# A decode attention kernel: VectorE's 30 middle heads as a loop, and value sums put ahead of the transposes that wait for a load

## Chip, cores, metric

One core of one Trainium2 chip. The metric is the device time of one execution in microseconds. Times before and after are medians. The profile of a kernel is that of one execution, and its span is some 1.8 us below that execution's time: 1927.44 us for the kernel before (a run beside those of the median).

## The reference, cut to what matters

One token (x is 1x640) attends to 32 heads of 32768 cached keys and values of 192 numbers each, in bf16, followed by a small dense block. K and V together are 805 MB, and each byte is used once.

```python
q = (layernorm(x) @ wq).reshape(1, 1, 32, 192).transpose(0, 2, 1, 3)
p = softmax(einsum("bhqd,bhkd->bhqk", q, k_cache) * 192 ** -0.5)      # 32 heads, 32768 keys
h = x + einsum("bhqk,bhkd->bhqd", p, v_cache)....reshape(1, 1, 6144) @ wo
out = h + relu(layernorm(h) @ w1) @ w2
```

## The kernel before

Each head's K and V come in 4 loads of 3 MB each; a load is worked on in two chunks of 32 columns of 128 keys. TensorE (PE) transposes 20 or 16 of the 32 columns, ScalarE (ACT) copies them out of PSUM, PE forms scores; VectorE (DVE) forms the scores of the other 12 or 16 columns by products and sums. ACT takes exponents (`ep`, `ed`), and PE sums the values. SyncE (SP) issues the loads; POOL turns landings into semaphore increments for PE. PE and ACT run heads 1 to 30 as a loop; DVE, POOL and SP are written out for all heads. In the lines of the profile `tp` are the transposes in PSUM (where this kernel puts PE's results), `kT` their copies, `sp` PE's scores, `pr` and `sc` VectorE's products and sums, `pB` and `pA` the exponents of `sp` and of `sc`, `o_ps` the value sums, `qb` the query row. The parts that matter (cuts marked):

```python
# SP: a V load waits for the value sums of the load before the last (2 V buffers, 4 K buffers)
load(kt[ld][:], rows(k_hd, h, ...), f"dk{ld}", "k", h, ld)
if n >= NV:
    hp, lp = divmod(n - NV, NL)
    g.wait("PV", hp, 2 * lp + 1)
load(vt[ld % NV][:], rows(v_hd, h, ...), f"dv{ld % NV}", "v", h, ld)
...
# PE: a new load's transposes (even c) wait for K; the values of the chunk before stand behind them
def pe_head(g, h, turn=None):
    for c in range(NC):
        transposes(g, h, c)
        if c > 0:
            values(g, h, c - 1)
        elif h > 0:
            values(g, h - 1, NC - 1)
            den_mm(g, h - 1)
        scores_pe(g, h, c)
        ...
# DVE: written out
def dve_program(g):
    ...
    for h in range(H):
        for c in range(len(chunks(h))):
            scores_dve(g, h, c)            # waits for the K load itself
            if c == 0 and h > 0:
                den_rec(g, h - 1)
                o_scale(g, h - 1)
            if c == 1 and h > 0:
                o_turned(g, h - 1)         # even h: memset of oT; odd h: a copy
```

The softmax here doesn't subtract the row's maximum and nothing guards it: scores larger than these inputs give would overflow.

## Time and profile before

| | before |
|---|---|
| time, median of the 3 runs then made | 1926.88 us |
| HBM traffic | 825 MB, 428 GB/s over the span, 433 in a good slice |
| PE, DVE, ACT busy | 81%, 80%, 50% |
| DVE instructions in the trace | 979, of which 670 counted as busy work |
| refill packets (the page's kind "instruction", queue q14; DVE's are 8192 bytes and stand 124 to 131 of its instructions apart) | 15 |

The page's view of the DMA issues tells how long a load takes from issue to landing (last column, us). At 433 GB/s a 3 MB load is 7.27 us of work, so 15.5 us says that about one load was still in front of a V load when it was issued.

```profile
kt<-in_A_k_cache_dram SPq DMA_DIRECT2D x127, 3072.0 KB, 22.5
vt<-in_A_v_cache_dram SPq DMA_DIRECT2D x127, 3072.0 KB, 15.5
```

The shares of the chain of waits that ended last:

```profile
DMA 76%; PE 22%; SPq 1%; issue 0%; ACT 0%; POOLq 0%; DVE 0%
```

### The profile page before, as it was taken

How to read it: one execution, taken by the hardware profiler on the slowest of the kernel's cores; microseconds unless marked ns; L12 is line 12 of the kernel's file. 1: busy time of each engine (PE TensorE's matmuls, PEld its weight loads, DVE VectorE, ACT ScalarE, POOL GpSimd, SP SyncE). 2: the span in 40 equal slices, each digit the busy share in tenths (PEclk: the TensorE clock that was granted, in tenths of full speed). 3: DMA queues.
4: the chain of work that ended last, by engine and by line, in shares of the span. 5: the costliest groups of instructions: out<-in, count | busy, mean ns of one | idle time of the engine just before them, and what ended most of it. 6: DMA issues, size and time to landing. Idle time of an engine off the chain costs nothing.

```text
span 1925.6 us, 36082 instructions
## 1 busy us (share of the span) xinstructions
PE 1563.4 (81%) x15899; PEld 1074.8 (56%) x15899; DVE 1546.3 (80%) x670; ACT 970.6 (50%) x2031; POOL 0.7 (0%) x6
## 2 busy tenths in 40 slices
PE   5887888787887888788788878888778888888788
PEld 4555555555555555555555555555555555555555
DVE  5888888787887888887788878888778887888786
ACT  4554555454554554555454554545445454545554
POOL 0000000000000000000000000000000000000000
PEclk8889888888989898888888888888888888898888
DMA  9999999999999999999999999999999999999997
GB/s 408 430 432 433 433 432 432 433 433 431 433 430 433 433 433 433 433 432 427 434 433 433 433 431 433 430 435 432 430 431 431 435 432 433 431 431 429 431 432 321
DMA packets 44799, 825.31 MB, mean 429 GB/s; under 512 B 4580, under 2 KB 6116, under 8 KB 12132
## 3 DMA queue, kind: packets, MB, share of 16 engines
q1 hardware_dynamic: 44762, 824.99, 99.8%
q8 instruction: 12, 0.20, 0.0%
q14 instruction: 15, 0.12, 0.0%
q10 hardware_dynamic: 10, 0.00, 0.0%
HBM read 824.97 MB, written 0.00 MB: 428 GB/s over the span
## 4 chain that ended last, share of the span: by engine, by line
DMA 76%; PE 22%; SPq 1%; issue 0%; ACT 0%; POOLq 0%; DVE 0%
DMA kt<-in_A_k_cache_dram 76%; PE o_ps L319 11%; PE tp L338 10%; SPq L221 1%; PE mm L319 1%; PE sp L319 0%; PE attT L319 0%; ACT kT L533 0%; POOLq L301 0%; DVE o_pair L631 0%; ACT pB L539 0%; PE mm L522 0%; ACT h1T L595 0%; DVE y_row L699 0%; DVE h_col L681 0%
## 5 line engine op out<-in xcount | busy, mean ns | idle before, releaser
L617 DVE TENSOR_TENSOR pr<-kt,qb 128x2304 f32<-128x2304 bf16 (+2 forms) x257 | 755.8, 2941 | 298.9 <-DMA kt<-in_A_k_cache_dram 282.6
L533 ACT COPY kT<-tp 128x1024 bf16<-128x1024 bf16 (+1 forms) x899 | 818.9, 992 | 342.2 <-PE tp L338 340.2
L338 PE MATMUL tp<-ident_f,kt 128*128 128x128 f32 x3459 | 571.7, 332 | 341.8 <-POOLq L301 341.8
L620 DVE TENSOR_REDUCE sc<-pr 128x12 f32<-128x2304 f32 (+2 forms) x257 | 755.3, 2939 | 8.9
L338 PEld LDWEIGHTS tp<-ident_f,kt 128*128 128x128 f32 x3459 | 498.1, 173 | 358.7 <-POOLq L301 357.5
L319 PE MATMUL o_ps<-vt,pB 128*2 128x384 bf16 x2286 | 470.9, 357 | 3.5 <-POOLq L301 3.4
L319 PE MATMUL o_ps<-vt,pA 128*2 128x384 bf16 x1778 | 331.0, 326 | 0.0
L319 PEld LDWEIGHTS o_ps<-vt,pB 128*2 128x2 bf16 x2286 | 184.1, 89 | 239.8 <-issue 87.6
L539 ACT ACTIVATE pB<-sp 128x20 bf16<-128x20 f32 (+2 forms) x258 | 47.9, 186 | 503.1 <-PE sp L319 503.1
L319 PEld LDWEIGHTS sp<-qm,kT 128*128 128x128 bf16 x6918 | 193.2, 97 | 77.7 <-issue 67.5
L319 PEld LDWEIGHTS o_ps<-vt,pA 128*2 128x2 bf16 x1778 | 151.0, 85 | 144.7 <-issue 8.1
L319 PE MATMUL sp<-qm,kT 128*128 128x2 bf16 x6918 | 212.0, 164 | 3.0 <-ACT kT L533 2.1
L548 ACT ACTIVATE pA<-sc 128x12 bf16<-128x12 f32 (+2 forms) x257 | 53.4, 208 | 89.0 <-DVEq L64 88.3
L539 ACT ACTIVATION_READ_ACCUMULATOR pB<-sp 128x1 f32 x258 | 50.2, 195 | 0.0
L548 ACT ACTIVATION_READ_ACCUMULATOR pA<-sc 128x1 f32 x257 | 48.7, 190 | 0.0
L625 DVE TENSOR_REDUCE rec<-mm 128x1 f32<-128x20 f32 x32 | 5.7, 179 | 51.6 <-PE mm L319 51.1
L319 PE MATMUL mm<-wq_s,xn_ln 128*1 (+1 forms) x160 | 18.7, 248 | 3.6 <-POOLq L301 3.6
L631 DVE TENSOR_SCALAR o_pair<-o_ps,rec 2x384 bf16<-2x384 f32 x32 | 19.4, 605 | 2.8 <-PE o_ps L319 1.7
L319 PE MATMUL attT<-oT,wo_s 128*128 128x1 bf16 x465 | 15.9, 163 | 0.3 <-DVE oT L638 0.3
L319 PEld LDWEIGHTS mm<-dsums,ones_mat 128*128 128x128 f32 x64 | 9.5, 188 | 10.7 <-issue 9.3
L319 PE MATMUL mm<-ones_row,row_e 1*128 1x1 bf16 x384 | 14.0, 159 | 0.0
L319 PEld LDWEIGHTS attT<-oT,wo_s 128*128 128x128 bf16 x465 | 13.8, 95 | 0.3 <-DVE oT L638 0.3
(69 smaller groups left out, 129.1 us busy)
## 6 DMA issues: line engine op xcount, KB each, us to landing
kt<-in_A_k_cache_dram SPq DMA_DIRECT2D x127, 3072.0 KB, 22.5
vt<-in_A_v_cache_dram SPq DMA_DIRECT2D x127, 3072.0 KB, 15.5
wq_s<-in_A_wq_dram SPq DMA_DIRECT2D x4, 1920.0 KB, 21.9
wo_s<-in_A_wo_dram SPq DMA_DIRECT2D x16, 480.0 KB, 16.3
kt<-in_A_k_cache_dram SPq DMA_DIRECT2D x1, 1920.0 KB, 19.7
kt<-in_A_v_cache_dram SPq DMA_DIRECT2D x2, 960.0 KB, 24.3
kt<-in_B_w_dram SPq DMA_DIRECT2D x1, 1920.0 KB, 18.3
wq_s<-in_B_w_dram SPq DMA_DIRECT2D x1, 960.0 KB, 20.3
```

The costliest lines, as they stand in the source:

```text
L221: g.do(lambda: nc.sync.dma_start(out=dst, in_=src), sem, label, by=16)
L319: return lambda: pe.matmul(o, lhsT=w, rhs=r, **kw)
L338: calls.append(lambda b=b, o=o: pe.transpose(out=dst[:, b, :], in_=src[:, o:o + 2 * P].bitcast(f32), identity=ident_f[:]))
L533: g.do(lambda: act.copy(out=kT[c % 2][:, b0:b0 + nb, :], in_=src[:, 0:nb, :].bitcast(bf16)), "act_pe", ("cp", h, c, k))
L539: g.do(lambda: act.activation(out=pB[c % 4][:, 0:jp], in_=sp[:, 0:jp], func=F.Exp, scale=SCALE, accum_out=dsums[:, 2 * c + 1:2 * c + 2]), ...
L548: g.do(lambda: act.activation(out=pA[c % 4][:, 0:jd], in_=sc[c % NC][:, 0:jd], func=F.Exp, scale=SCALE, accum_out=dsums[:, 2 * c:2 * c + 1 ...
L617: g.chain(lambda: dve.tensor_tensor(out=pr[:, 0:j1 - j0, :], in0=src[:, (off + j0) * Dh:(off + j1) * Dh].rearrange("p (j d) -> p j d", d=D ...
L620: g.chain(lambda: dve.reduce_sum(out=sc[c % NC][:, j0:j1], in_=pr[:, 0:j1 - j0, :], axis=X), "dve")
L625: g.chain(lambda: dve.reduce_sum(out=rec[:, 0:1], in_=mm[:, 0:2 * NCM], axis=X), "dve")
L631: g.do(lambda: dve.tensor_scalar_mul(out=o_pair[:, :, h % 2, :], in0=o_ps[0:2, 0:2 * Dh].rearrange("q (i d) -> q i d", i=2), scalar1=rec[0 ...
```

## The change

The intent: (1) DVE's heads 1 to 30 become a loop like PE's and ACT's. A loop needs the same instructions in each head, so the even/odd difference becomes a number (`odd`, toggled 1 and 0), the head before last is carried by a copy of `o_pair`, and DVE's waits get their own semaphores that can be counted down per head (DMA landings reach it through POOL, PE's results through `pe_dve`). (2) On PE the value sums of an odd chunk are put ahead of the next load's transposes, so that they run while PE would wait for K; the last head's end is reordered too.

```diff
+    def pe_chunk(g, h, c):
+        if c % 2 == 1:
+            transposes(g, h, c)
+        if c > 0:
+            values(g, h, c - 1)
+        elif h > 0:
+            values(g, h - 1, NC - 1)
+            den_mm(g, h - 1)
+        if c % 2 == 0:
+            transposes(g, h, c)
+        scores_pe(g, h, c)
 ...                                  # the end of head 31, E0 = 6
         transposes(g, h, E0)
+        transposes(g, h, E0 + 1)
         values(g, h, E0 - 1)
-        for c in range(E0 + 1, NCM):
-            transposes(g, h, c)
-            scores_pe(g, h, c - 1)
-            if c > E0 + 1:
-                values(g, h, c - 2)
+        scores_pe(g, h, E0)
+        transposes(g, h, E0 + 2)
+        scores_pe(g, h, E0 + 1)
+        values(g, h, E0)
 ...
-        g.wait("k", h, ld)
+            g.wait("atd", "k", h, ld)          # DVE: by POOL's relay
 ...
-        if h % 2 == 1:
-            g.do(lambda: dve.tensor_copy(out=oT[:], in_=mm[:, 0:3]), "dve_pe", ("oTc", h))
-        else:
-            g.do(lambda: dve.memset(oT[:], 0.0), "dve_pe", ("oTc", h))
+        g.do(lambda: dve.tensor_scalar_mul(out=oT[:], in0=mm[:, 0:3], scalar1=odd[:]), "dve_pe", ("oTc", h))
+        if h < LAST:
+            g.chain(lambda: dve.tensor_copy(out=o_pair[:, :, 0, :], in_=o_pair[:, :, 1, :]), "dve")
 ...
-            dve_program(Program(book, sems, nc.vector))
+            looped("dve", nc.vector)
```

More of the change, by code (lines that the diff above doesn't have):

```diff
@@ L26, in __init__ @@
         self.log = []
-        self.links = 0
+        self.links = {}
     def wait(self, *label):
@@ L46, in chain @@
     def chain(self, fn, sem, label=None):
-        if self.links > 0:
-            self.wait("link", sem, self.links)
-        self.links += 1
+        n = self.links.get(sem, 0)
+        if n > 0:
+            self.wait("link", sem, n)
+        self.links[sem] = n + 1
         self.row = sem
-        self.do(fn, sem, ("link", sem, self.links))
+        self.do(fn, sem, ("link", sem, n + 1))
         if label is not None and self.planning:
-            self.book["at"][label] = self.book["at"]["link", sem, self.links]
+            self.book["at"][label] = self.book["at"]["link", sem, n + 1]
     def tell(self, sem, label):
-        self.wait("link", self.row, self.links)
+        self.wait("link", self.row, self.links[self.row])
         if self.planning:
@@ L175 @@
     oT = sbuf("oT", [P, 3], bf16)
+    odd = sbuf("odd", [P, 1], f32)
     x_col = sbuf("x_col", [P, DT], f32)
@@ L208, in v_tile @@
         return v_at[(h, ld)] if (h, ld) in v_at else vt[ld % NV][:]
-    names = ["pool_pe", "act_pe", "dve_pe", "act_dve", "dve_act", "dve", "pool_dve", "pool_act", "pe_act", "pe"]
+    names = ["pool_pe", "act_pe", "dve_pe", "act_dve", "dve_act", "dve", "dve_row", "pe_dve", "pool_row", "pool_dve", "pool_act", "pe_act", "pe"]
     names += [f"dk{i}" for i in range(NL)] + [f"dv{i}" for i in range(NV)] + ["dwq", "dwo", "dx", "dout"]
@@ L214 @@
     sems = {n: nc.alloc_semaphore(n) for n in names}
-    TAKEN = {"pe": ("pool_pe", "act_pe", "dve_pe"), "act": ("pe_act", "dve_act")}
+    TAKEN = {"pe": ("pool_pe", "act_pe", "dve_pe"), "act": ("pe_act", "dve_act"),
+             "dve": ("pool_dve", "act_dve", "pe_dve", "dve")}
     def dma_program(g):
@@ L278, in pool_program @@
         g.do(lambda: e.affine_select(out=ident_b[:], in_=ident_b[:], compare_op=A.not_equal, fill=1.0, base=0,
-                                     pattern=[[-1, P]], channel_multiplier=1), "pool_dve", ("ident",))
+                                     pattern=[[-1, P]], channel_multiplier=1), "pool_row", ("ident",))
         g.wait("x")
@@ L286, in pool_program @@
                 relay(g, "k", h, ld)
+                g.do(lambda: nc.gpsimd.sem_inc(sems["pool_dve"], 1))
+                book_relay(g, "k", h, ld, sem="pool_dve")
                 relay(g, "v", h, ld)
@@ L302, in relay, with book_relay @@
         book_relay(g, *label)
-    def book_relay(g, *label):
+    def book_relay(g, *label, sem="pool_pe"):
         if g.planning:
-            n = g.book["count"].get("pool_pe", 0) + 1
-            g.book["count"]["pool_pe"] = n
-            g.book["at"][("at",) + label] = ("pool_pe", n)
+            n = g.book["count"].get(sem, 0) + 1
+            g.book["count"][sem] = n
+            g.book["at"][("at" if sem == "pool_pe" else "atd",) + label] = (sem, n)
     pe = nc.tensor
@@ L403, in den_mm @@
             g.wait("oTc", h - 1)
-        pe_group(g, [mmul(mm[:, 0:2 * NCM], ones_mat[:], dsums[:], start=True, stop=True)], ("den", h))
+        pe_group(g, [mmul(mm[:, 0:2 * NCM], ones_mat[:], dsums[:], start=True, stop=True)], ("den", h), "pe_dve")
     def o_turn(g, h):
@@ L410, in o_turn @@
         pe_group(g, [mmul(mm[:, b:b + 1], rows[i][:, b:2 * Dh:3], ident_b[0:2, i:i + 1],
-                          start=(i == 0), stop=(i == 1)) for b in range(3) for i in range(2)], ("oT", h))
+                          start=(i == 0), stop=(i == 1)) for b in range(3) for i in range(2)], ("oT", h), "pe_dve")
     def project(g, h):
@@ L442, in q_spread @@
         pe_group(g, calls, ("qs", h), "pe_act")
+    def pe_chunk(g, h, c):
[9 more added lines that the diff above has]
+        scores_pe(g, h, c)
     def pe_head(g, h, turn=None):
         for c in range(NC):
-            transposes(g, h, c)
-            if c > 0:
-                values(g, h, c - 1)
-            elif h > 0:
-                values(g, h - 1, NC - 1)
-                den_mm(g, h - 1)
-            scores_pe(g, h, c)
+            pe_chunk(g, h, c)
             if c == 1 and h > 0:
@@ L463, in pe_norm @@
         g.wait("st", "ln1")
-        pe_group(g, [mmul(mm[:, 0:2], mean_mat[:], ln_t["ln1"]["st"][:], start=True, stop=True)], ("mean", "ln1"))
+        pe_group(g, [mmul(mm[:, 0:2], mean_mat[:], ln_t["ln1"]["st"][:], start=True, stop=True)], ("mean", "ln1"), "pe_dve")
     def pe_start(g):
@@ L469, in pe_start @@
         pe_group(g, [lambda: pe.transpose(out=mm[:, 0:4].bitcast(bf16)[:, 0:DT], in_=x_row[:],
-                                          identity=ident_b[0:DT, 0:DT])], ("xT",))
+                                          identity=ident_b[0:DT, 0:DT])], ("xT",), "pe_dve")
         pe_norm(g)
@@ L482, in pe_end @@
         for c in range(E0):
-            transposes(g, h, c)
-            if c > 0:
-                values(g, h, c - 1)
-            else:
-                values(g, h - 1, NC - 1)
-                den_mm(g, h - 1)
-            scores_pe(g, h, c)
+            pe_chunk(g, h, c)
             if c == 1:
@@ L492, in pe_end @@
         transposes(g, h, E0)
+        transposes(g, h, E0 + 1)
         values(g, h, E0 - 1)
-        for c in range(E0 + 1, NCM):
-            transposes(g, h, c)
-            scores_pe(g, h, c - 1)
-            if c > E0 + 1:
-                values(g, h, c - 2)
+        scores_pe(g, h, E0)
+        transposes(g, h, E0 + 2)
+        scores_pe(g, h, E0 + 1)
+        values(g, h, E0)
+        transposes(g, h, E0 + 3)
+        scores_pe(g, h, E0 + 2)
+        values(g, h, E0 + 1)
         scores_pe(g, h, NCM - 1)
@@ L506, in pe_end @@
         g.wait("h_col")
-        pe_group(g, [mmul(mm[:, 0:1], mean_mat[:], st[:, 0:1], start=True, stop=True)], ("mean", "ln2"))
+        pe_group(g, [mmul(mm[:, 0:1], mean_mat[:], st[:, 0:1], start=True, stop=True)], ("mean", "ln2"), "pe_dve")
         g.wait("st", "ln2")
-        pe_group(g, [mmul(sp[:, 0:2], mean_mat[:], st[:], start=True, stop=True)], ("mean2",))
+        pe_group(g, [mmul(sp[:, 0:2], mean_mat[:], st[:], start=True, stop=True)], ("mean2",), "pe_dve")
         g.wait("xn", "ln2")
@@ L519, in pe_end @@
                               start=(f == 0 and n == 0), stop=(f == FT - 1 and n == DT - 1), skip_group_check=True)
-                         for f in range(f0, f1) for n in range(DT)], ("y", i))
+                         for f in range(f0, f1) for n in range(DT)], ("y", i), "pe_dve")
         g.wait("y_col")
-        pe_group(g, [lambda: pe.transpose(out=mm[0:DT, 0:P], in_=y_col[:], identity=ident_f[:])], ("yT",))
+        pe_group(g, [lambda: pe.transpose(out=mm[0:DT, 0:P], in_=y_col[:], identity=ident_f[:])], ("yT",), "pe_dve")
     act = nc.scalar
@@ L605, in scores_dve @@
             return
-        g.wait("k", h, ld)
+        if h == LAST and ld >= NL - 1:
+            g.wait("k", h, ld)
+        else:
+            g.wait("atd", "k", h, ld)
         if c == 0:
             g.wait("qb", h)
-            if h > 0:
-                g.wait("PV", h - 1, 1)
         if h == LAST and c >= NC:
@@ L628, in o_scale @@
     def o_scale(g, h):
-        g.wait("PV", h, len(chunks(h)) - 1)
+        if h == LAST:
+            g.wait("PV", h, NCM - 1)
         g.wait("rec", h)
-        g.do(lambda: dve.tensor_scalar_mul(out=o_pair[:, :, h % 2, :],
+        g.do(lambda: dve.tensor_scalar_mul(out=o_pair[:, :, 1, :],
                                            in0=o_ps[0:2, 0:2 * Dh].rearrange("q (i d) -> q i d", i=2),
@@ L635, in o_turned @@
     def o_turned(g, h):
+        g.chain(lambda: dve.tensor_scalar(out=odd[:], in0=odd[:], scalar1=-1.0, scalar2=1.0, op0=A.mult, op1=A.add),
+                "dve", ("odd", h))
         g.wait("oT", h)
-        if h % 2 == 1:
-            g.do(lambda: dve.tensor_copy(out=oT[:], in_=mm[:, 0:3]), "dve_pe", ("oTc", h))
-        else:
-            g.do(lambda: dve.memset(oT[:], 0.0), "dve_pe", ("oTc", h))
+        g.wait("odd", h)
+        g.do(lambda: dve.tensor_scalar_mul(out=oT[:], in0=mm[:, 0:3], scalar1=odd[:]), "dve_pe", ("oTc", h))
+        if h < LAST:
+            g.chain(lambda: dve.tensor_copy(out=o_pair[:, :, 0, :], in_=o_pair[:, :, 1, :]), "dve")
     def dve_norm(g, tag, col):
         t = ln_t[tag]
-        g.chain(lambda: dve.reduce_sum(out=t["st"][:, 0:1], in_=col[:], axis=X), "dve")
+        g.chain(lambda: dve.reduce_sum(out=t["st"][:, 0:1], in_=col[:], axis=X), "dve_row")
         g.chain(lambda: dve.scalar_tensor_tensor(out=t["sq"][:], in0=col[:], scalar=1.0, in1=col[:], op0=A.mult,
-                                              op1=A.mult, accum_out=t["st"][:, 1:2]), "dve", ("st", tag))
+                                              op1=A.mult, accum_out=t["st"][:, 1:2]), "dve_row", ("st", tag))
         g.wait("mean", tag)
-        g.chain(lambda: dve.tensor_copy(out=t["mv"][:], in_=mm[:, 0:2]), "dve")
+        g.chain(lambda: dve.tensor_copy(out=t["mv"][:], in_=mm[:, 0:2]), "dve_row")
         g.chain(lambda: dve.scalar_tensor_tensor(out=t["nv"][:], in0=t["mv"][:, 0:1], scalar=t["mv"][:, 0:1],
-                                              in1=t["mv"][:, 1:2], op0=A.mult, op1=A.subtract), "dve")
+                                              in1=t["mv"][:, 1:2], op0=A.mult, op1=A.subtract), "dve_row")
         g.tell("dve_act", ("nv", tag))
         g.wait("sd", tag)
-        g.chain(lambda: dve.reciprocal(out=t["rs"][:], in_=t["sd"][:]), "dve", ("rs", tag))
+        g.chain(lambda: dve.reciprocal(out=t["rs"][:], in_=t["sd"][:]), "dve_row", ("rs", tag))
         g.wait("rs", tag)
@@ L656, in dve_norm, with dve_start @@
                                        op0=A.subtract, op1=A.mult), "dve_pe", ("xn", tag))
-    def dve_program(g):
+    def dve_start(g):
         for t, v in ((ones_row, 1.0), (mean_mat, 1.0 / D), (eps_t, eps), (row_e, 0.0), (ones_mat, 1.0), (dsums, 0.0),
-                     (o_pair, 0.0), (zero5, 0.0), (oT, 0.0)):
-            g.chain(lambda: dve.memset(t[:], v), "dve")
+                     (o_pair, 0.0), (zero5, 0.0), (oT, 0.0), (odd, 1.0)):
+            g.chain(lambda: dve.memset(t[:], v), "dve_row")
         g.wait("ident")
@@ L664, in dve_program, with dve_head, dve_end @@
         g.wait("xT")
-        g.chain(lambda: dve.tensor_copy(out=x_col[:], in_=mm[:, 0:4].bitcast(bf16)[:, 0:DT]), "dve")
+        g.chain(lambda: dve.tensor_copy(out=x_col[:], in_=mm[:, 0:4].bitcast(bf16)[:, 0:DT]), "dve_row")
         dve_norm(g, "ln1", x_col)
-        for h in range(H):
-            for c in range(len(chunks(h))):
-                scores_dve(g, h, c)
-                if c == 0 and h > 0:
-                    den_rec(g, h - 1)
-                    o_scale(g, h - 1)
-                if c == 1 and h > 0:
-                    o_turned(g, h - 1)
+    def dve_head(g, h):
+        for c in range(len(chunks(h))):
+            scores_dve(g, h, c)
+            if c == 0 and h > 0:
+                den_rec(g, h - 1)
+                o_scale(g, h - 1)
+            if c == 1 and h > 0:
+                o_turned(g, h - 1)
+    def dve_end(g):
         h = LAST
+        dve_head(g, h)
         den_rec(g, h)
@@ L681, in dve_program @@
         g.chain(lambda: dve.scalar_tensor_tensor(out=h_col[:], in0=attT[:, 0:DT], scalar=1.0, in1=x_col[:], op0=A.mult,
-                                                 op1=A.add, accum_out=t["st"][:, 0:1]), "dve", ("h_col",))
+                                                 op1=A.add, accum_out=t["st"][:, 0:1]), "dve_row", ("h_col",))
         g.chain(lambda: dve.scalar_tensor_tensor(out=t["sq"][:], in0=h_col[:], scalar=1.0, in1=h_col[:], op0=A.mult,
-                                                 op1=A.mult, accum_out=t["st"][:, 1:2]), "dve", ("st", "ln2"))
+                                                 op1=A.mult, accum_out=t["st"][:, 1:2]), "dve_row", ("st", "ln2"))
         g.wait("mean", "ln2")
@@ L688, in dve_program @@
         g.wait("mean2")
-        g.chain(lambda: dve.tensor_copy(out=t["mv"][:], in_=sp[:, 0:2]), "dve")
+        g.chain(lambda: dve.tensor_copy(out=t["mv"][:], in_=sp[:, 0:2]), "dve_row")
         g.chain(lambda: dve.scalar_tensor_tensor(out=t["nv"][:], in0=t["mv"][:, 0:1], scalar=t["mv"][:, 0:1],
-                                                 in1=t["mv"][:, 1:2], op0=A.mult, op1=A.subtract), "dve")
+                                                 in1=t["mv"][:, 1:2], op0=A.mult, op1=A.subtract), "dve_row")
         g.tell("dve_act", ("nv", "ln2"))
         g.wait("sd", "ln2")
-        g.chain(lambda: dve.reciprocal(out=t["rs"][:], in_=t["sd"][:]), "dve")
+        g.chain(lambda: dve.reciprocal(out=t["rs"][:], in_=t["sd"][:]), "dve_row")
         g.tell("dve_act", ("rs", "ln2"))
@@ L698, in dve_program @@
         g.wait("yT")
-        g.do(lambda: dve.tensor_copy(out=y_row[:], in_=mm[0:DT, 0:P]), "dve", ("y_row",))
+        g.do(lambda: dve.tensor_copy(out=y_row[:], in_=mm[0:DT, 0:P]), "dve_row", ("y_row",))
     book = {"count": {}, "at": {}}
     plan = Program(book, sems)
-    for f in (dma_program, pool_program, dve_program):
+    for f in (dma_program, pool_program):
         f(plan)
-    parts = {"pe": (pe_start, pe_head, pe_end), "act": (act_start, act_head, act_end)}
-    logs = {}
+    parts = {"pe": (pe_start, pe_head, pe_end), "act": (act_start, act_head, act_end), "dve": (dve_start, dve_head, dve_end)}
+    logs, links = {}, {}
     for e, (start, head, end) in parts.items():
         logs[e] = []
+        plan = Program(book, sems)
         for h in range(LAST):
@@ L716 @@
         plan.log = []
+        links[e] = dict(plan.links)
         end(plan)
@@ L741, in take @@
         def take(amounts):
+            g.flush()
             for s, n in amounts.items():
@@ L756, in looped @@
             g.sub[s] = g.seen[s] = ends_at[e][LAST - 1][s]
+        g.links = dict(links[e])
         end(g)
```

## The prediction

Its sum came to 2.7 + 1.1 - 0.3 = 3.5 us, from 1926.9 to 1923.4. That all seven mid-run refills of DVE would go was the author's estimate; for it the trace of before has PE's loop, with none of its packets (q8) from 123.6 to 1861.5 us. A load shows 16 increments in the trace and the page counts 16 DMA engines; that each increment is one engine's is the author's reading. Where one engine is said to be behind, the measured thing is that the last increment alone is late (5.33 us after the first, with the others within 1.01, in the landing of 1747.22). The 0.7 us for one of POOL's refills was an estimate.

> **What bounds the kernel now.** I read the page's first three parts first, to see whether an engine or the loads set the pace.
>
> ```profile
> PE 1563.4 (81%) x15899; PEld 1074.8 (56%) x15899; DVE 1546.3 (80%) x670; ACT 970.6 (50%) x2031; POOL 0.7 (0%) x6
> ...
> DMA  9999999999999999999999999999999999999997
> GB/s 408 430 432 433 433 432 432 433 433 431 433 430 433 433 433 433 433 432 427 434 433 433 433 431 433 430 435 432 430 431 431 435 432 433 431 431 429 431 432 321
> DMA packets 44799, 825.31 MB, mean 429 GB/s; under 512 B 4580, under 2 KB 6116, under 8 KB 12132
> ...
> q1 hardware_dynamic: 44762, 824.99, 99.8%
> q8 instruction: 12, 0.20, 0.0%
> q14 instruction: 15, 0.12, 0.0%
> ```
>
> No engine reaches 9 tenths; the DMA engines are full in every slice but the last. 825.31 MB at the 433 GB/s of a good slice is 1906 us, and the page's span is 1925.6. So everything that any change to the compute order can win is about 20 us (1%), in the first microseconds, the tail, and whatever keeps the loads under 433. A gain of 2% (38.5 us) would need fewer bytes; the change removes none of the cache.
>
> Next, the waits by total and the DMA queue's own waits, then the chain of waits in the last 46 us.
>
> ```profile
> PE tp L338 <- POOLq L301: 341.8, 127, 7.2
> ...
> DVE pr L617 <- DMA kt<-in_A_k_cache_dram: 282.6, 108, 9.3
> ...
> SPq L221 <- PE o_ps L319: 1320.5, 95, 34.1
> ...
> 1864.26 22.41 DMA kt<-in_A_k_cache_dram
> ...
> 1886.77 3.46 PE tp L338 x15
> 1890.23 4.01 PE o_ps L319 x16
> ...
> 1919.31 0.28 ACT h1T L595
> ...
> 1922.02 0.28 DVE y_row L699
> ```
>
> PE and DVE wait for K at nearly every load (341.8/127 = 2.7 us each), so both have slack. The queue's 1320.5 us of waiting for value sums looks like a bottleneck and is not one: the V load of 557.39 us is issued while the K load of 543.17 us still has 8.3 us to go (it lands at 565.66), so the engines do not run dry. The end hangs on K load 2 of head 31: issued 1864.26, landed 1886.67, then 39 us of tail.
>
> What decides "landed"? A load counts as landed with its 16th increment. I took the 16 increment times from the trace's semaphore events (us after the first of the 16):
>
> ```
> landed 98.09:   0 .11 .12 .13 .17 .25 .28 .31 .34 .37 .73 1.48 1.54 1.57 1.73 1.77
> landed 616.56:  0 .19 .20 .23 .29 .48 .53 .58 1.37 1.42 1.43 1.46 1.48 1.56 1.58 1.69
> landed 624.78:  0 .17 .20 .23 .26 .49 .56 .62 1.38 1.43 1.44 1.47 1.49 1.58 1.63 2.65
> landed 1747.22: 0 .20 .29 .43 .50 .51 .61 .69 .80 .86 .87 .90 .92 1.00 1.01 5.33
> landed 1886.67: 0 .16 .17 .23 .26 .39 .40 .49 .68 1.06 1.10 1.13 1.23 2.16 2.67 4.59
> ```
>
> One DMA engine falls behind its fifteen peers by 0.85 to 0.95 us at a time, near 100, 364, 619, 884, 1154, 1410 and 1675 us, and ends 4.3 us behind all the others. At those seven times the packet records hold an 8192-byte q14 "instruction" packet (99.7, 363.8, 618.9, 883.9, 1153.9, 1409.9, 1674.9). Counting instructions executed up to each, DVE stands at 64, 192, 318, 448, 579, 703, 831: steps of 128[...]. These are DVE's refills. POOL's steps of 128 fit 323.0, 1082.6 and 1845.7, SP's fit 501.4 and 1375.1. ACT and PE already loop; PE's 16 KB packets stand only before 124 us and from 1861 us.
>
> [...]
>
> **The change part by part.**
>
> 1. DVE loops over heads 1 to 30. Its straight program is 979 instructions (7.6 packets of 128). Start, head 0, one body, head 31 and end come to an estimated 190[...]. The seven mid-run refills go: 0.06 MB (0.14 us of bandwidth, nothing), but the one late engine falls back into the pack: 7 x 0.88 = 6.1 us of lag go, and it was 4.59 behind the first. The landing is then set by the next engine. At 1886.67 that one is at 2.67, so 1.92 earlier. Also, the fifteen quick engines were held up near 1755 us and 1815 us: the last one's lag fell from 5.34 to 4.89 and 4.98 to 4.57 while its own loads kept their 7.27 us step, so the others lost 0.45 + 0.3 = 0.75 us. They ran out of work because the V load waits for value sums that wait for the late engine. Without a late engine that goes too: K load 2 lands 1.92 + 0.75 = 2.7 us earlier.
>
> 2. POOL relays each K load to DVE: 127 more semaphore instructions, one more refill on POOL's engine (about 0.7 us), which stands in the middle of the pack: 0. DVE hears of K some 0.1 us later.
>
> 3. Value sums of odd chunks before the transposes that wait for K. In the steady state PE does 2.9 us of work in a wait of 2.7 us, the V load is issued some 3 us earlier, and the queue, already never empty, gets deeper: 0. In the tail it counts once: after K load 2, PE runs transposes 3.46, values 4.01, scores. Now the values start when the last exponents are there (DVE's sums end about 2.5 us before K), take up to 4 us on a slow PE and hold the transposes some 1.8 us; afterwards the scores wait for ACT's copies of the transposes (about 1 us), which the values hid. Net about 4.0 - 1.8 - 1.1 = 1.1 us.
>
> 4. The end's reorder (two transposes, then values). Today scores at 1906.62 wait for 2.2 us of copies that stand ahead of an exponent on ACT; that order hides them better, but the second transposes wait for a PSUM tile. About 0.3 us lost to 0.8 won; I take 0.3 lost. DVE's own chain after K (sums to 1909.81) has some 1 us to spare, so it allows this gain and not much more.
>
> 5. DVE additions per head: a toggle (0.16), a scaled copy in place of a memset (0.16 against 0.06), a 2x384 copy (about 0.4): 0.7 us in a head that leaves 4 x 2.7 us: 0 on the path. Branch and register work at the head's edge falls into the K wait (ACT's branch took 45 ns): 0.
>
> Sum: 2.7 + 1.1 - 0.3 = 3.5 us; 1926.9 - 3.5 = 1923.4 us. The w1 and w2 loads land by 1913.41 and 1919.32, needed about 1917.6 and 1921.06, and are pulled forward as K is, so they do not take over.
>
> **The rivals.**
>
> *Loads hidden anyway, no gain at all.* If refills are only moved, or another engine takes the last place at once (PE's 16 KB packets at 1861 and 1876 already pushed one to 2.67), 1.9 us shrink to 0 and the time is 1925 to 1927. For it: the page's DMA share is 99.8%. Against it: the lag at 1747 was one engine alone.
>
> *The tail wins more.* If the values run before K at full speed (2.9 us, as in the steady state) the tail gives 2 to 3 us: 1921. Against it: DVE's 23 us of products and sums after K load 2, which do not move.
>
> *A new wait makes it slower.* DVE's extra ops come at chunk 1, where DVE ends only 0.1 us before K (memset at 565.58, K at 565.66), and the odd chunk's values now stand ahead of the transposes and wait for it. Each head would lose 0.6 us and win it back within one load, as every load leaves 2.7 us. If it did not, 31 x 0.6 = 19 us: 1942, still 1%.
>
> **Range and chances.** All of it is within 10 us, so within 2% is near certain. The centre is 1923.4; the low end 1920.5 adds the second rival, the high end 1926.3 is the first. Neither a gain nor a loss of 38 us has a mechanism, save an unforeseen stall in the new loop: 1% for slower, and under 1% for faster.
>
> **What would show it.** Right: no 8 KB q14 packets at 128-instruction steps of DVE, the 16 increments within about 2 to 2.7 us of each other late in the run, K load 2 of head 31 landing near 1884, GB/s unchanged at 431 to 433, K and V times from issue to landing longer by 2 to 4 us because they are issued earlier, PE's wait for POOL smaller, the tail after that landing near 38 us. Wrong: a spread that stays at 4 us (refills were not its cause), a landing at 1886 in spite of a small spread (the loads are bound by the total rate, not by the last engine), slices below 430 GB/s (the deeper queue disturbs), or DVE idle growing at the head's edge.

## The result

| | before | after |
|---|---|---|
| time, median of 4 runs | 1926.99 us (1926.21 to 1927.18) | 1924.13 us (1923.81 to 1924.93) |
| profiled span | 1925.6 us | 1923.1 us |
| K load 2 of head 31 landed | 1886.67 | 1883.87 |
| from there to the span's end | 38.9 | 39.2 |
| its 16 increments within | 4.59 | 3.22 |

The ratio is 0.9987, interval 0.9969 to 1.0004. Ratios here are the mean time of one kernel's fast runs over that of the other's of the same rounds, so not quite the ratio of the medians that stand beside them. The difference of 2.9 us is seen in each run, as the two ranges do not touch, and in the landing.

The page of the changed kernel, the same lines as shown of before:

```profile
PE 1523.1 (79%) x15899; PEld 1028.9 (54%) x15899; DVE 1560.5 (81%) x734; ACT 965.7 (50%) x2031; POOL 0.7 (0%) x6
...
GB/s 408 429 432 432 433 433 432 433 432 432 433 430 433 434 433 432 431 433 427 436 431 434 432 432 431 433 433 434 429 433 432 433 432 433 433 431 432 432 432 334
...
q1 hardware_dynamic: 44762, 824.99, 99.9%
q8 instruction: 12, 0.20, 0.0%
q14 instruction: 10, 0.07, 0.0%
...
PE 49%; DMA 23%; ACT 17%; DVE 9%; issue 1%; SPq 0%; ACTq 0%; DVEq 0%; POOLq 0%
...
kt<-in_A_k_cache_dram SPq DMA_DIRECT2D x127, 3072.0 KB, 26.9
vt<-in_A_v_cache_dram SPq DMA_DIRECT2D x127, 3072.0 KB, 19.9
```

The rate is the same, and so are the bytes but for the refills: of 15 packets of 8192 bytes 9 are left (the page's tenth has 72 bytes). By the instructions executed up to each, DVE has one for eight (seven in mid-run and one at 1917.3 us before) and POOL four for three. Loads are issued 4.4 us earlier relative to their landing (26.9 for 22.5, 19.9 for 15.5), and nothing comes of it: e1 below, with 22.5 and 15.5 again, is as fast. The chain that ended last no longer hangs on the loads (DMA 23% for 76%) but on PE's own order of work, which step 3 below takes up. The page's waits have turned round completely:

```profile
PEld sp L324 <- ACT kT L542: 337.5, 127, 2.7
PE sp L324 <- ACT kT L542: 307.5, 127, 2.4
...
PE o_ps L324 <- ACT pA L557: 64.3, 103, 2.5
DVE pr L627 <- ACT qb L568: 55.7, 13, 6.0
```

PE's 341.8 us of waiting for K before transposes are 11.7 us now (page group of the transposes), and in their place stand 307.5 us before the scores, for ACT's copies of those transposes, which the value sums used to cover, and 64.3 us before the values, for the exponents. DVE has a new wait, for the query row, in 13 heads.

The increments of one load's landing, from the trace's semaphore events (us after the first of the 16):

```
after, landed 1743.10:  0 .09 .14 .29 .38 .64 .87 1.42 1.47 1.48 1.53 1.62 1.68 1.69 1.70 1.79
after, landed 1853.34:  0 .10 .14 .29 .38 .64 .87 1.42 1.47 1.49 1.53 1.63 1.68 1.69 1.71 1.78
after, landed 1883.87:  0 .15 .29 .38 .64 .87 1.42 1.46 1.48 1.53 1.63 1.69 1.71 1.79 2.36 3.22
```

The engine that stood 5.33 us behind at 1747 us is back in the pack. What pushes the last place out between 1853 and 1884 are, by their times, PE's two 16 KB packets as its loop ends (1857.7, 1872.9) and one of POOL's 8 KB packets (1857.5).

### The profile page after: what moved, and what is told of

Its sections match the earlier page's. It is cut to its first block, busy times and chain, and to the rows that moved or that the text cites. A ratio compares the mean times of both kernels' runs of the same rounds, so it can differ in the third digit from the quotient of the medians.

```text
span 1923.1 us, 36522 instructions
## 1 busy us (share of the span) xinstructions
PE 1523.1 (79%) x15899; PEld 1028.9 (54%) x15899; DVE 1560.5 (81%) x734; ACT 965.7 (50%) x2031; POOL 0.7 (0%) x6
## 4 chain that ended last, share of the span: by engine, by line
PE 49%; DMA 23%; ACT 17%; DVE 9%; issue 1%; SPq 0%; ACTq 0%; DVEq 0%; POOLq 0%
PE o_ps L324 28%; DMA kt<-in_A_k_cache_dram 22%; ACT kT L542 15%; PE tp L343 12%; PE sp L324 7%; DVE sc L630 4%; DVE pr L627 4%; ACT pA L557 1%; DMA vt<-in_A_v_cache_dram 1%; PE mm L324 1%; ACT pB L548 1%; PE attT L324 1%; SPq L224 0%; DVE o_pair L642 0%; DVE rec L635 0%
## 5 line engine op out<-in xcount | busy, mean ns | idle before, releaser
L343 PE MATMUL tp<-ident_f,kt 128*128 128x128 f32 x3459 | 520.0, 311 | 11.7 <-POOLq L306 11.3
L324 PE MATMUL o_ps<-vt,pB 128*2 128x384 bf16 x2286 | 467.3, 355 | 66.7 <-ACT pA L557 64.3
L343 PEld LDWEIGHTS tp<-ident_f,kt 128*128 128x128 f32 x3459 | 451.8, 161 | 45.3 <-issue 30.9
L324 PE MATMUL sp<-qm,kT 128*128 128x2 bf16 x6918 | 214.7, 164 | 307.5 <-ACT kT L542 307.5
L652 DVE TENSOR_SCALAR oT<-mm,odd 128x3 bf16<-128x3 f32 x32 | 7.1, 223 | 17.0 <-PE mm L324 15.5
L324 PEld LDWEIGHTS mm<-ones_row,row_e 1*128 1x128 bf16 x384 | 15.5, 99 | 0.2
## 6 DMA issues: line engine op xcount, KB each, us to landing
kt<-in_A_k_cache_dram SPq DMA_DIRECT2D x127, 3072.0 KB, 26.9
vt<-in_A_v_cache_dram SPq DMA_DIRECT2D x127, 3072.0 KB, 19.9
```

The costliest lines, as they stand in the source:

```text
L324: return lambda: pe.matmul(o, lhsT=w, rhs=r, **kw)
L343: calls.append(lambda b=b, o=o: pe.transpose(out=dst[:, b, :], in_=src[:, o:o + 2 * P].bitcast(f32), identity=ident_f[:]))
L652: g.do(lambda: dve.tensor_scalar_mul(out=oT[:], in0=mm[:, 0:3], scalar1=odd[:]), "dve_pe", ("oTc", h))
```

## The experiments

Eight runs in two groups of four, each group on one chip with the kernel before beside it (median of before 1926.27 in the first group, 1926.48 in the second). "Landing" is that of K load 2 of head 31, "tail" the time from there to the span's end. The rows of the increments can't show which engine is which; that one and the same engine is hit is read from the last place alone growing.

### e1: the loop without the new order

The edit in words:

```diff
-    pe_chunk: odd c: transposes, values, scores; even c: values, transposes, scores
+    pe_chunk: transposes, values, scores for every c; end of head 31 as before
```

> The changed kernel with the order of before on PE everywhere (transposes always ahead of the values); only VectorE's loop, the relays and the small VectorE additions are left. Theory (the seven VectorE refills held one DMA engine back and the loop alone gives the gain): no 8 KB refills at VectorE's steps, increments of one load within 2 us of each other until 1850 us, K load 2 of head 31 lands at 1883.5 to 1885, tail after it 38.9 as before, time 1923.5 to 1925. Rival A (the earlier V loads of the new order gave the gain): landing back at 1886 to 1887 and 1926 to 1928 in spite of the loop.

Measured: 1924.03 us (1923.70 to 1924.83), ratio 0.9988; landing 1883.88, increments within 1.9 us at 1743 us and 3.09 at the landing, tail 38.0. PE's waits are those of before again:

```profile
PEld tp L343 <- POOLq L306: 351.4, 127, 7.1
PE tp L343 <- POOLq L306: 335.7, 127, 7.1
...
DVE pr L621 <- POOLq L290: 267.9, 105, 9.7
```

So the loop alone gives the whole gain (2.2 us against before; the changed kernel again, e8, 2.4), with PE waiting for K as it ever did. Rival A has fallen. The tail is 0.9 us shorter than the 38.9 expected; step 3 says why that is no gain of the loop.

### e2: the new order without the loop

The edit, shortened:

```diff
-            looped("dve", nc.vector)
+            dve_start(g); dve_head(g, h) for h in 0..30; dve_end(g)     # written out
```

> The changed kernel with VectorE's program written out for all heads again (1109 instructions, 128 more than before, because of the toggle, the copy and their semaphore work); the new PE order stays. Theory: about eight mid-run refills, one engine 5.5 to 6.5 us behind the first by 1750 us, its fifteen peers not held up any more (no step down of the lag near 1755 and 1815 us) because V is issued earlier, K load 2 of head 31 lands at 1886.5 to 1887.5, time 1926.5 to 1928.5: the new order without the loop gains nothing. Rival A (order gives the gain): 1924 to 1925.

Measured: 1929.62 us (1928.59 to 1930.88), ratio 1.0017, so it is slower than before, by some 3 us, and 1 us more than expected. Eight DVE packets (93.6, 321.3, 561.9, 790.5, 1021.1, 1243.1, 1476.4, 1708.6 us), one engine behind by 6.87 us:

```
e2, landed 1748.25:  0 .06 .25 .44 .46 .86 1.07 1.31 1.41 1.46 1.51 1.55 1.56 1.56 1.57 6.87
e2, landed 1887.58:  0 .05 .24 .45 .85 1.06 1.45 1.51 1.53 1.55 1.56 1.57 2.00 2.13 2.86 6.85
```

The landing, 1887.58, is 0.1 us past the expected range; the tail is 39.8 us, longer than the changed kernel's 39.2. Two things follow. The order gains nothing by itself. And it does what it was made for: the first of the sixteen increments comes at 1880.73, as in the changed kernel (1880.65), against 1882.08 in the kernel before; the fifteen quick engines are never held up (taking off the weight loads in between, no load-to-load step of the first increment is more than 0.25 us over 7.27), although the late one is later than ever. Only, nobody asks for the first increment.

### e3: e2 with more DVE instructions

```diff
         g.tell("dve_act", ("sc", h, c))
+        if not g.planning and 0 < h < LAST:
+            for _ in range(4):
+                nc.vector.sem_inc(sems["pad"], 1)
```

> e2 with 32 more semaphore increments per head on VectorE (2069 instructions, 960 more, on a semaphore nobody waits for). Theory: 7.5 more refills of 128 instructions, each 0.85 to 0.95 us on the same DMA engine, so its lag reaches 12 to 13 us, K load 2 of head 31 lands 6 to 7 us later than in e2, time 6 to 7 us over e2 (1933 to 1935). Rival B (what matters is the bytes, or the total rate, and the late engine only rearranges the landings): within 1 us of e2. Rival C (the added instructions cost by VectorE's own time): VectorE idle before its products shrinks by 2 us a head but stays over 5 us a head, so no effect by this road.

Measured: 1938.32 us (1937.94 to 1941.22), ratio 1.0065; landing 1896.30, 8.7 us after e2's. Sixteen DVE packets stand before the landing for e2's eight. Reading the step from one landing to the next (7.27 us when nothing happens), the last increment is late by 0.95 to 1.04 us after each of the twelve from 563.6 us on (the first four cost less, while their engine is not yet the last). Eight more at 0.97 is 7.8 us; the remaining 1.0 us is lost at 1201.8 and 1224.3 us (0.33 and 0.67), where there is no packet: there the quick engines ran 3.6 us late in three loads, for want of issued work (the V load of 1200.20 was issued 0.66 us before the first of them was done with the load ahead), and even the late one was touched. It is the page's dip:

```profile
GB/s 406 431 430 433 434 432 432 432 430 433 433 432 432 431 434 432 432 433 430 433 431 432 435 432 415 416 423 432 430 433 432 431 433 432 433 416 426 431 431 292
```

So the time rose by 8.7 us in step with the landing where 6 to 7 were expected: the mechanism held. Missed was that the lag would reach 12 to 13 us: it is 7.5 us at the landing, since the quick engines were held up too. And a packet costs 0.96 us on the last increment, not the 0.88 that the differences between neighbours in one landing had given. Rivals B and C have fallen: the added bytes are 0.06 MB (0.14 us of bandwidth), and DVE's idle time had room.

### e4: PE kept busy in the tail's new wait

```diff
+        if h == LAST and c == NC - 4:
+            for _ in range(40):
+                g.do(mmul(mm[:, 256:384], ident_b[:], ident_b[:], start=True, stop=True))
         scores_pe(g, h, c)
```

> The changed kernel with 40 matmuls of a 128x128 identity into unused columns of a bank, put into the wait of 2.4 us before the scores of chunk 4 of head 31 (1886.4 to 1888.8 us), the result of which nobody reads. Theory (the tail's expected gain of 0.8 us was lost because PE's clock fell to half in that wait): granted clock 1.0 after it in place of 0.5, the next 12 transposes take 1.5 us in place of 2.8, the next values 2.7 in place of 4.2, the end comes 1.3 to 2.2 us earlier, 1922 to 1923. Rival D (the tail is bound by VectorE's products and sums, which end 23.3 us after K load 2): the transposes and values get faster but the last values end as before, 1924.

Measured: 1923.84 us (1923.69 to 1923.89), ratio 0.9986; landing 1883.68, tail 38.3. The windows of the changed kernel over transposes, scores, transposes and values after the landing (columns: window, its length, PE busy with instructions, granted clock, which is the share of its full clock that PE was given, DMA share, GB/s), then those of e4:

```profile
1884.50:1886.40 1.90, 1.88 (x16) 1.00 1.02 440
1888.80:1889.70 0.90, 0.88 (x31) 0.50 1.01 432
1889.70:1892.40 2.70, 2.70 (x17) 0.50 0.97 414
1892.40:1896.60 4.20, 4.20 (x18) 0.64 0.99 411
```

```profile
1886.20:1887.80 1.60, 1.60 (x16) 1.00 0.98 424
1890.50:1891.20 0.70, 0.70 (x29) 1.00 0.85 363
1891.20:1892.70 1.50, 1.50 (x20) 1.00 1.02 432
1892.70:1895.40 2.70, 2.70 (x18) 1.00 0.96 404
```

The clock and the two durations came as expected (12 transposes 1.5 for 2.8 us, values 2.7 for 4.2). The end did not come 1.3 us sooner, because head 31 started late here: DVE waited 5.73 us for the query row at 1855.73 (in the changed kernel's profile 4.25 us), everything after ran 1.6 us later, and the 2.8 us won shrank to about 1. That the clock, lost in the wait, made these transposes and values slow is thus shown; that it is worth a gain in the time is not (0.3 us against the changed kernel, 0.2 against e8 on another chip).

### e5: PE kept busy ahead of the transposes, in the order of before

```diff
+        if h == LAST and c == NC - 4:
+            for _ in range(40):
+                g.do(mmul(mm[:, 256:384], ident_b[:], ident_b[:], start=True, stop=True))
         transposes(g, h, c)            # e1 otherwise
```

> e1 (VectorE's loop, PE order of before) with 40 matmuls of the identity, read by nobody, put ahead of the transposes of K load 2 of head 31, where PE waits some 2.8 us for that load. Theory (the tail's length is set by PE's clock after its waits): clock 1.0 at those transposes in place of 0.5, they take 1.9 us in place of 3.4, the end comes 1 to 1.5 us after K load 2 sooner than in e1 (38.0 us there), so 36.5 to 37 us, time 1922 to 1923. Rival D (VectorE's 23.3 us after the load bound the tail): 38 us stay, 1924.

Measured: 1923.91 us (1923.58 to 1924.60), ratio 0.9987; landing 1883.89, tail 38.0: rival D's number, but not its reason. The transposes took 1.86 us in place of 3.41, and PE began the next chunk's value sums 1.1 us earlier than in e1_loop_old_order; then the chain of waits goes back to another load:

```profile
1874.93 20.82 DMA kt<-in_A_k_cache_dram
1895.76 0.04 issue
1895.80 1.20 PE tp L343 x9
1897.00 2.69 PE o_ps L324 x16
```

The last K loads of head 31 begin to land at 1895.76, and PE waits 1.06 us for the first of them. The gain in the tail became a new wait.

### e6: more POOL instructions, in e1

```diff
                 relay(g, "v", h, ld)
+                if 0 < h < LAST:
+                    for _ in range(10):
+                        g.do(lambda: nc.gpsimd.sem_inc(sems["pad"], 1))
```

> e1 with 40 more semaphore increments per head on POOL, which nobody waits for (1200 instructions, 9.4 more refills), its relays unchanged. Theory (any sequencer's straight code holds one DMA engine back, 0.85 to 0.95 us a refill, whichever sequencer it is): one engine, POOL's, gets 6 to 8 us behind the pack, K load 2 of head 31 lands 6 to 8 us later than in e1, time 1930 to 1932. Rival E (only VectorE's refills matter, because VectorE stalls while it waits for its instructions): 1924 to 1925, no lag.

Measured: 1928.16 us (1927.20 to 1928.26), ratio 1.0007; landing 1887.46, 3.6 us after e1's; q14 packets of 8192 bytes 18 against 9.

```
e6, landed 1747.58:  0 .42 .58 .67 .76 .77 .81 .96 1.15 1.16 1.17 1.31 1.33 1.33 1.34 5.59
```

One engine alone falls behind, at each of POOL's packets from 680 us on (680.5, 827.6, 965.8, 1104.8, 1244.7, 1385.7, 1530.3, 1670.1, 1810.0), the last increment later by 0.63 to 0.70 us each time. Rival E has fallen: POOL holds no compute work, and its refills do the same. The size was missed: a POOL packet costs 0.65 us, a DVE packet 0.96, both being 8192 bytes and 0.31 us long in the records; and four of its packets are spent before its engine becomes the last. Why the two differ stays open.

### e7: PE kept busy in every such wait

```diff
+        if c % 2 == 0:
+            for _ in range(5):
+                g.do(mmul(sp[:, 256:384], ones_mat[:], ident_f[:], start=True, stop=True))
         scores_pe(g, h, c)
```

The matmuls write unused columns of the scores' bank; the exponents that read that bank are waited for by the values just ahead.

> The changed kernel with 5 idle f32 matmuls into unused columns of the scores' bank ahead of the scores of every even chunk, where PE waits 2.4 us for ACT's copies (307 us in all). Theory: PE keeps its full clock, VectorE's new waits for the query row (55.7 us over 13 heads, because the row comes late after a slow PE) go to nearly 0, but none of this is on the path of the loads, so the landing of K load 2 stays at 1883 to 1884.5; the tail gets shorter by 1.5 to 2.5 us since head 31 starts on time and with a full clock: 1922 to 1923. Rival F (PE's slow stretches held the V loads back): landing earlier by over 1 us and the GB/s up.

Measured: 1924.62 us (1924.01 to 1925.41), ratio 0.9990; landing 1883.99; tail 39.0. The mean granted clock rose to 0.949 from 0.91. DVE's wait for the query row is down from 42.1 us in 11 heads in e8, or 55.7 in 13, to one of 3.4 us:

```profile
DVE pr L630 <- ACT qb L571: 3.4, 1, 3.4
```

The landing did not move, so neither these waits nor PE's slow stretches are on the loads' path; rival F has fallen. The tail did not shorten, and the time is 1.6 us past the expected range: the five matmuls took 1.28 us of the wait, and the 12 transposes after it took 2.75 us, about as long as in the changed kernel at clock 0.50 (2.80).

### e8: the changed kernel again

> The changed kernel itself once more, unchanged, for a comparison on one chip with e5, e6 and e7: 1923.5 to 1925, K load 2 of head 31 lands at 1883.5 to 1884.5, tail 38.5 to 39.5.

Measured: 1924.07 us (1923.70 to 1926.29), ratio 0.9990; landing 1884.03, tail 38.2, 0.3 short of the expected range. So the tail of the same program differs by 1 us from one profile to the next (39.2 before), and differences of half a microsecond between e1, e4, e5, e7 and e8 are not to be read. None of them beats the changed kernel clear of noise.

## Why the prediction was right, point by point

**The bound.** Right: bytes and rate are unchanged, and 1924.13 us lies in the range, 0.7 us over the centre.

**Step 1, the refills.** Right, and shown from both sides: taken away (e1) 2.2 us go, doubled (e3) 8.7 us come, on another engine (e6) 4.1 us come over e1 and 1.7 over before. Six of the seven mid-run refills went, not all: one is left at 86.1 us, where DVE stands at its 64th instruction as it did at 99.7 us before, and none of DVE's follows it in the loop or after; at 1743 us no engine stands apart. In the packet records the refills of DVE, POOL and SP stand on q14 with 8192 bytes each, PE's on q8 (12 packets of 16 KB; before, those up to 123.6 us come in steps of some 260 PE instructions, weight loads counted). The landing moved by 2.80 us, where 2.7 was said, but that is luck: its two terms were mis-sized and made up for each other. The late engine's distance to the first fell from 4.59 to 3.22, so 1.37 and not 1.92, since one of POOL's packets at 1857.5 and PE's at 1857.7 and 1872.9 pushed the last place further. The first increment came 1.43 us earlier, not 0.75; in the kernel before its loads are late by 0.30, 0.45 and 0.41 us at 1432.7, 1756.9 and 1815.5 us. The first of these had not been counted, and the last, 4.98 to 4.57 by the prediction's own figures, was taken as 0.3.

**Step 2, POOL's relays.** Nothing until the end, as said (in the landing of K load 2 of head 31 DVE began 0.15 us after it, 0.03 before); the one more packet that fell at 1857.5 is the exception above. That POOL stands in mid-pack was right only for four packets: e6 gives it more, and it becomes the last.

**Step 3, values ahead of transposes.** Zero in the steady state was right (e1 against the changed kernel: 1924.03 and 1924.13). In the tail the 1.1 us did not come in the profile of the changed kernel: this is the term of the sum that failed. The values did not hold the transposes for 1.8 us but for 0.65 (they took 2.76 us at full clock), and the first scores came 4.95 us after the landing in place of 7.57, 2.6 us won. All of it was given back at once: PE had now 2.44 us with nothing to do, its clock fell to 0.50, and the next transposes and values took 2.66 and 4.20 us in place of 1.38 and 2.69 (from the chain of waits, before and after). The prediction had put the slow stretch in the same place as before the change; here it came after PE's new wait, and e4 shows that by filling it. How long it lasts is luck: in e8, the same program, the transposes took 2.66 us again but the values only 2.94, which is most of the 1 us between the two tails; and in e1 it took in the transposes alone (3.41), not the values (2.76 for 4.01 before), hence its 38.0 (e6, with the same loop and order, has 3.73 and 38.8). The changed kernel's clock records give 0.50 from 1888.64 us on, within that wait of 2.44 us and after 1.9 us of transposes, for 6.83 us; from 1861.33 us on its stretches of one clock last 3.41, 23.89, 6.83 and 20.48 us, multiples of 3.41. In the wait at that place 1.28 us of f32 matmuls left the next 12 transposes at 2.75 us (e7), while 2.40 us of bf16 matmuls brought them to 1.51 us at clock 1.00 (e4).

Not in the sum at all: with the new order the transposes no longer start when K load 2 has landed. They stand behind values that wait for exponents (1881.83 below), and begin 0.65 us after the landing here, 0.8 in e8, 1.6 in e7 and 2.5 in e4, where head 31 ran late; with the old order it was 0.10. The chain that ended last is 76 to 77% DMA in before, e1, e5 and e6, and 22 to 29% in after, e2, e3, e4 and e8 (44% in e7). So, by these chains, a still earlier landing alone would not shorten the changed kernel's end; no run tests it.

**Step 4, the end's reorder.** About as said: in the second transposes the chain passes 1.94 us of ACT's copies, which free the PSUM tile for the last transpose (ACT kT 1897.86, PE tp 1899.84); in the kernel before it passed 2.20 us of copies, at 1904.19. The steps are seen in the chain but no run separates them.

```profile
1881.83 2.76 PE o_ps L324 x16
1884.59 0.60 PE tp L343 x4
...
1885.22 3.56 ACT kT L542 x4
...
1888.82 0.96 PE sp L324 x30
1889.78 2.66 PE tp L343 x12
1892.44 4.20 PE o_ps L324 x16
...
1897.86 1.94 ACT kT L542 x2
```

**Step 5, DVE's additions.** Off the path, as said. Measured in head 31: toggle 0.15, scaled copy 0.22, copy of `o_pair` 0.24 us. (The 0.16 and 0.06 us of the prediction are the copy and the memset of `oT` before, 0.164 and 0.061; its 0.4 us was an estimate.) What was not foreseen is the wait for the query row: the row is made by PE after the scores of chunk 6 and taken by ACT behind the exponents of chunk 7, and a PE at half clock there makes it late (clock 0.50 from 1845 to 1850 us in the changed kernel, ahead of the wait of 4.25 us; with a mean clock of 0.949 in e7 one wait of 3.4 us is left).

**The rivals.** "Loads hidden anyway" was wrong by the landing, and right in that PE's late packets took part of the gain. "The tail wins more" failed for the clock and, in e5, for the next K load, not for DVE. "A new wait makes it slower" is half true: the waits came (307.5 and 64.3 us on PE, 55.7 on DVE) and cost nothing outside the tail (e7 took DVE's away, and the landing stayed).

## What to carry to other kernels

When a kernel is bound by loads at the rate of a good slice (433 GB/s here), look at the increments of one landing: a load counts as landed with the last of its 16, and in the kernel before that one alone ran up to 5.34 us behind the first. The instruction refills of DVE, whose program was written out for all heads, held the last increment back and added up: 0.96 us for each 8192-byte packet, or 128 instructions (e3), once it was clear of the rest; the loop won back what lay beyond the next-latest, 2.8 us of the landing, and no more. Work moved into a wait on an engine off the path changed nothing in the steady state but the names of the waits; at the end it put that engine on the path, and the clock was 0.50 for what came next (1.00 in e4, with the wait filled).
